# Another order of states, scalings and x operands in the projection phase of the last eight chunks

## The chip, the cores and the metric

The kernel runs on one core of a Trainium2 chip. The metric is device time in microseconds, as the median of three runs of the whole kernel: 601.86 (601.72 to 603.16).

## What is computed

Linear attention with a decay, block by block, feeds a feed-forward layer with a squared ReLU. All inputs and outputs are float32.

```python
# attention: batch 4, heads 8, 768 tokens, 64 per head, blocks of 64
for b in range(nb):
    intra = np.einsum('bhic,bhjc->bhij', qb, kb) * Dmask[None]
    intra = np.einsum('bhij,bhjd->bhid', intra, vb)
    inter = np.einsum('bhid,bhde->bhie', qb * lam_pow[None], kv_state)
    out[:, :, sl] = intra + inter
    kb_dec = kb * rev_pow[None]
    kv_state = lam_block * kv_state + np.einsum('bhsd,bhse->bhde', kb_dec, vb)
# feed-forward: 3072 tokens, d_model 512, d_ff 2048
h = x @ w_in
r = np.maximum(h, 0.0)
return ((r * r) @ w_out).astype(np.float32)
```

## The kernel before

**Tiling.** Tokens go in 24 chunks of 128, six per batch row; a chunk holds all eight heads, two by two in four pairs. Chunks 0 to 7 make the first two groups of the feed-forward, chunks 8 to 15 the next two, chunks 16 to 23 the last two. Every float32 factor of a matrix product is kept as a rounded high part and a remainder (`wh` and `wl`, `gh` and `gl`, `xh` and `xl`), and a product is three matmuls. From the third group on the products go by a scheme with seven products instead of eight (`product`, line 667; `gather`, line 897), which wants sums of blocks of the weights and of x as operands.

**Order.** Nothing is scheduled by a program: each engine runs its instructions in the order in which the code emits them, and waits where an operand is not there. The engines are TensorE (PE), VectorE (DVE), ScalarE (ACT), GpSimd (POOL) and SyncE (SP), which issues the DMAs.

**The projection phase of the last eight chunks** is the loop over f from 0 to 15 behind the `quad` loop. At its start all hidden values of group m are done, and one projection of it is left; those of group m + 1 lie in `gs`. Each step f does one projection (`project`: 24 matmuls from lines 537, 538 and 542 into four `acc` banks). It needs `gh` (ACT, line 960) and `gl` (DVE, line 522), which `again` makes from `gs` one step ahead, in two buffers each. Each even step also does the attention of one chunk t = 16 + f/2, by `go(t, after, apart)`. That is on PE: the old states times the queries (line 442), the scores of chunk t + 1 (line 406), the new parts of the state (`news_of`, line 421) and the masked scores times the values (line 467). Ahead of line 467 stands a copy of one element on ACT, `mark` (line 447): line 467 may add to its bank only when that copy has read it. Behind it ACT copies the result to `packs` (line 478), and DVE masks the scores of t + 1 (`a`).

The state of a chunk has two halves. `state(t, False)` adds the decayed state `kvd` and the new part for the first half of t + 1; `state(t + 1, True)` does the same for its second half; each runs on DVE (`kv`), and POOL then decays the result (`fade_state`, line 496, `kvd`). `scale_q(t + 1)` and `scale_k(t + 2)` are POOL operations on the queries and keys in place (lines 398 and 390). go(t + 1) reads both states, the queries of t + 1 and the keys of t + 2.

Two chunks at a time are also turned into operands x of the next phase: `even` and `last` are the chunks' results as they are, `near` and `far` are sums of DVE. `part_hi` rounds one on ACT (line 631), `part_lo` takes the remainder on DVE (line 635). The last two pairs of `w_out` rows get their sums here: `fold` (DVE: two `rec`, four `sums`), `fold_hi` (ACT, line 694), `fold_lo` (DVE, and two stores `wt` on SP, line 700). After the loop `open_ring` loads the first `ring` tiles, and `quad_all` starts the next phase.

At the very start chunks 0 to 3 are attended while `w_in` is taken apart: `clamp`, `shift`, `sign` and `rounded` are steps of that on DVE, and `masked(3)` makes `a` of chunk 3.

Of the kernel before, what the change touches and what calls it, by code (L numbers as in the profile page):

```python
# [24 lines left out]
NF = DF // P  # L25
# [10 lines left out]
def body(ctx: ExitStack, tc: tile.TileContext, qT, kT, kvq, lam, w, out):  # L36
# [43 lines left out]
    def load_kv(t):  # L80
        if t in (2, 3):
            x = lent[t][:, 1].rearrange("p a b -> p (a b)")
        elif t in lent:
            x = lent[t][:, 1]
        else:
            x = io.tile([P, 2 * DM], F32, name="kv_sb")
        nc.sync.dma_start(out=x, in_=kvq[t, :, 0 : 2 * DM])
        x = x.rearrange("p (k h d) -> p k h d", k=2, h=H)
        tok[t] = x[:, 0], x[:, 1]
# [50 lines left out]
    def sign(u):  # L140
        L, Hw, A = cv[u]
        V.scalar_tensor_tensor(  # L142
            out=A, in0=Hw, scalar=0xC0000000, in1=A, op0=ALU.bitwise_and, op1=ALU.bitwise_or
        )
# [153 lines left out]
    def masked(t):  # L298
        a_of[t] = []
        for j in range(2):  # L300
            a = wk.tile([P, NPR, C], F32, name="a", tag="gl" if t in (1, 3) else "a")
            V.tensor_tensor(
                out=a, in0=sc_of[t][j].rearrange("p (a b) -> p a b", a=NPR),
                in1=mask[:, j], op=ALU.mult,
            )
            a_of[t].append(a)
# [85 lines left out]
    def scale_q(t):  # L392
        x = feat[t][:, 1].rearrange("p a (b c) -> p a b c", b=2)
        if t % NCB:
            y = qpow[:, :, 0:D].unsqueeze(2).broadcast_to([P, NPR, 2, D])
        else:
            x, y = x[:, :, 1], qpow[:, :, 0:D]
        nc.gpsimd.tensor_tensor(out=x, in0=x, in1=y, op=ALU.mult)
# [33 lines left out]
    def go(t, after, apart):  # L432
        o = [ps_a.tile([P, DM], F32, name="att") for _ in range(2)]
        q_, vs = feat[t][:, 1], tok[t][1]
        for g in range(2):
            for p in range(NPR):
                for j, r in enumerate(rows):
                    h = (g + j + 1) % 2
                    if h and not t % NCB:
                        continue  # L440
                    st = kv[:, :, 0:D] if h else kv[:, :, D:]
                    nc.tensor.matmul(  # L442
                        o[h][r, p * D : (p + 1) * D], st[r, p, :], q_[r, p, of_half(h)],
                        start=p == 0, stop=False, skip_group_check=True,
                    )
                    end = h
        nc.scalar.copy(mark[:, 2:3], o[end][D : D + 1, 0:1])
        u = o
        if after is not None:
            scores_by_half(after, ps_h, "h")  # L450
            if apart:
                u = sc_of[after]

        def all_news():
            for p in range(NPR):
                if t % NCB < NCB - 1:
                    news_of(0, t, u[0], p, apart)
                if after is not None:
                    news_of(1, after, u[1], p, apart)

        if apart:
            all_news()
        a = a_of.pop(t)
        for p in range(NPR):
            for h in (end, 1 - end):
                for j, r in enumerate(rows):
                    nc.tensor.matmul(  # L467
                        o[h][r, p * D : (p + 1) * D], vs[rows[h], 2 * p + j, :], a[rows[h], j, p, :],
                        start=p == 0 and h == 1 and not t % NCB, stop=True, skip_group_check=True,
                    )  # L470
        if not apart:
            all_news()
        if after is not None:
            part_of[after] = u[1]
            masked_by_half(after)
        x = kept(t).rearrange("p (a c) -> p a c", a=NPR)
        for h in range(2):
            nc.scalar.copy(x[:, :, of_half(h)], o[h][:, 0 : NPR * D].rearrange("p (a c) -> p a c", a=NPR))
        part_of[t] = u[0]
# [48 lines left out]
    def project(m, f):  # L528
        gh, gl = g_of.pop((m, f))
        if f == 0:  # L530
            accs[m] = [ps_acc.tile([P, DM], F32, name="acc") for _ in range(G)]
        end = f == NF - 1
        j = w_out(f)

        def high(i):
            cs = slice(i * C, (i + 1) * C)
            nc.tensor.matmul(accs[m][i], gh[:, cs], wh[:, j], start=f == 0, stop=False)  # L537
            nc.tensor.matmul(accs[m][i], gh[:, cs], wl[:, j], start=False, stop=False)  # L538

        def low(i):  # L540
            cs = slice(i * C, (i + 1) * C)
            nc.tensor.matmul(accs[m][i], gl[:, cs], wh[:, j], start=False, stop=end)  # L542
            if end:
                if i % 2 == 0:
                    stage.append(wk.tile([P, 2, DM], F32, name="o", tag="A"))
                o = stage[-1][:, i % 2]
                if i % 2:
                    V.tensor_copy(o, accs[m][i])
                else:
                    nc.scalar.copy(o, accs[m][i])  # L550
                t = chunk(m, i)
                nc.sync.dma_start(out=out[t * C : (t + 1) * C, :], in_=o)

        n = 2 if end and m == NM - 1 else 1
        for i in range(0, G, n):
            for step in (high, low):
                for k in range(i, i + n):
                    step(k)
# [78 lines left out]
    def part(*a):  # L637
        part_hi(*a)
        part_lo(*a)

    def even(i, t):
        return i, 0, 4, kept(t)

    def last(i, t):
        return i, 4, 2, kept(t + 1)[:, 2 * C :]
# [33 lines left out]
    def fold(n):  # L679
        rec = wk.tile([P, 2, 2, 2 * P], F32, name="rec", tag="A")  # L680
        for i in range(2):
            j = w_out(2 * n + i)
            add(rec[:, i].rearrange("p b c -> p (b c)"), f32(wh[:, j]), f32(wl[:, j]))
        x = wk.tile([P, 4, 2 * P], F32, name="sums", tag="A")
        (b11, b12), (b21, b22) = ([rec[:, i, j] for j in range(2)] for i in range(2))
        T1, T2, T3, T4 = (x[:, i] for i in range(4))
        sub(T1, b12, b11)
        sub(T2, b22, T1)
        sub(T3, b22, b12)
        sub(T4, b21, T2)  # L690
        FOLD[n] = x

    def fold_hi(n):
        nc.scalar.copy(wh[:, NF - 2 : NF].rearrange("p a d -> p (a d)"), FOLD[n].rearrange("p a b -> p (a b)"))

    def fold_lo(n):
        hi, lo = (t[:, NF - 2 : NF].rearrange("p a d -> p (a d)") for t in (wh, wl))
        sub(lo, FOLD.pop(n).rearrange("p a b -> p (a b)"), f32(hi))
        for i, x in enumerate((hi, lo)):
            nc.sync.dma_start(out=wt[n, :, :, i], in_=f32(x).rearrange("p (a b) -> p a b", a=4))  # L700
# [280 lines left out]
    def att(t, pool, name):  # L981
        o[t] = pool.tile([P, DM], F32, name=name)
        u[t] = pool.tile([P, DM], F32, name=name)
# [21 lines left out]
    masked(2)  # L1005
    clamp(1)
    shift(1)
    sign(1)
    low[1] = split(1, o[1])
    scores(3, ps_acc, "acc")  # L1010
    prep_q(3)
    prep_k(3)
    masked(3)
    att(2, ps_a, "att")
    news(2, u[2])
    faded(2, u[2])
# [90 lines left out]
    def behind(f, t, last):  # L1107
        if f % 2:
            state(t, False)
            if t < last:  # L1110
                scale_q(t + 1)

    def ahead(f, t, last):
        if f % 2 and t < last:
            state(t + 1, True)
            if t + 2 <= last:
                scale_k(t + 2)
# [71 lines left out]
    masked_by_half(first_t)  # L1189
    state(first_t, True)  # L1190
    scale_q(first_t)
    for f in range(NF):
        t = first_t + f // 2
        i, odd_ = f // 4, f // 2 % 2
        project(*prev)
        prev = (m + 1, f)
        if f % 2 == 0:
            KEPT[t] = packs[:, i % 2, odd_]
            go(t, t + 1 if t < last_t else None, t < last_t)
            if t + 3 <= last_t:  # L1200
                load_qk(t + 3)
                load_kv(t + 3)
        if f + 1 < NF:
            again(m + 1, f + 1)
        if f % 2 == 0:
            behind(f + 1, t, last_t)
        else:
            ahead(f, t, last_t)
        if f in (4, 8):
            fold(NF // 2 - 2 + f // 8)  # L1210
        if f in (5, 9):
            fold_hi(NF // 2 - 2 + f // 8)
            fold_lo(NF // 2 - 2 + f // 8)
        if f % 4 == 1:
            part(*even(i, t))
        if f % 4 == 2:
            part(*near(i, t - 1))
        if f % 4 == 3:
            part(*far(i, t - 1))
            part(*last(i, t - 1))  # L1220
    open_ring()
    for n in range(NF // 2):
        quad_all(n, prev)
# [55 lines left out]
```

## Time and profile before

| | |
|---|---|
| median of three runs | 601.86 us |
| the profiled execution, whole | 602.65 us |
| its span, first to last instruction | 600.9 us |
| PE busy | 580.5 us (97%) |
| DVE busy | 421.9 us (70%) |
| ACT busy | 257.7 us (43%) |
| POOL busy | 100.4 us (17%) |
| the phase: go(16) to the first product behind it | 362.82 to 436.35 us |

Times in the profile are microseconds from the start of the span. An engine's idle time is put down to what released it. A matmul's duration in the trace is longer than its distance to the next one, since matmuls are pipelined; for PE the distances between starts tell the pace.

### The profile page before, as it was taken

The numbers are of one execution on the slowest core, as the hardware profiler recorded it, in microseconds if no ns is written. First come the engines' busy times: TensorE is split into PE (matmuls) and PEld (weight loads), VectorE is DVE, ScalarE is ACT, GpSimd is POOL, SyncE is SP. The second block draws the span as 40 slices with busy tenths as digits, with TensorE's granted clock in tenths as the row PEclk, the third lists the DMA queues.
The fourth block names the chain that finished last, engine by engine and source line by source line (L and its number), as shares of the span: only waits on it lengthen the run. The fifth ranks groups of instructions, "written<-read, shape, count | busy, mean of one in ns | idle before, by whom it ended". The sixth has DMA issues, their size and how long they took to land.

```text
span 600.9 us, 12444 instructions
## 1 busy us (share of the span) xinstructions
PE 580.5 (97%) x5006; PEld 491.2 (82%) x5006; DVE 421.9 (70%) x684; ACT 257.7 (43%) x437; POOL 100.4 (17%) x106
## 2 busy tenths in 40 slices
PE   7989999999999999999999999888899999999996
PEld 5777888888888888888888888676788888999996
DVE  6899999947656758566666645878664546997942
ACT  4576877734334455433333323333342323642520
POOL 5421222333323231000000013344200000000000
PEclk9999999999999999999999999999999999999999
DMA  8766576328788692656666555255058666766863
GB/s 299 271 236 211 160 260 212 106 71 289 233 284 270 212 320 81 192 150 195 194 192 194 177 179 183 100 182 171 3 190 291 195 194 181 244 209 211 282 204 114
DMA packets 69385, 119.31 MB, mean 199 GB/s; under 512 B 6352, under 2 KB 30928, under 8 KB 69328
## 3 DMA queue, kind: packets, MB, share of 16 engines
q1 hardware_dynamic: 67152, 116.42, 59.7%
q10 hardware_dynamic: 2176, 2.10, 1.0%
q8 instruction: 40, 0.66, 0.5%
q14 instruction: 17, 0.14, 0.1%
HBM read 88.08 MB, written 29.36 MB: 195 GB/s over the span
## 4 chain that ended last, share of the span: by engine, by line
PE 77%; DVE 12%; ACT 3%; issue 3%; POOL 2%; DMA 2%; SPq 0%; DVEq 0%; POOLq 0%
PE h L667 17%; PE h L507 12%; PE acc L897 7%; PE acc L537 7%; PE acc L542 7%; PE acc L538 7%; PE att L667 7%; PE att L897 4%; PE h L897 2%; PE att L442 2%; PE att L467 1%; DVE A L142 1%; DVE far L212 1%; DVE sums L212 1%; DVE gl L522 1%
## 5 line engine op out<-in xcount | busy, mean ns | idle before, releaser
L537 PE MATMUL acc<-wh,gh 128*128 128x512 f32 x256 | 101.2, 395 | 0.0
L538 PE MATMUL acc<-wl,gh 128*128 128x512 f32 x256 | 99.8, 390 | 0.0
L542 PE MATMUL acc<-wh,gl 128*128 128x512 f32 x256 | 99.8, 390 | 0.0
L667 PE MATMUL h<-wh,ring 128*128 128x512 f32 x320 | 85.9, 390 | 0.0
L514 ACT ACTIVATE h<-h 128x512 f32<-128x512 f32 x48 | 28.0, 583 | 112.2 <-PE h L507 50.7
L667 PEld LDWEIGHTS h<-wh,ring 128*128 128x128 f32 x320 | 59.8, 188 | 13.2 <-DVE kv_sb L212 0.7
L522 DVE TENSOR_TENSOR gl<-h,gh 128x512 fp32r<-128x512 f32 x48 | 33.0, 688 | 39.6 <-ACT h L517 39.6
L537 PEld LDWEIGHTS acc<-wh,gh 128*128 128x128 f32 x256 | 48.0, 188 | 11.0 <-issue 0.3
L542 PEld LDWEIGHTS acc<-wh,gl 128*128 128x128 f32 x256 | 48.0, 188 | 10.6 <-DVE gl L522 0.5
L538 PEld LDWEIGHTS acc<-wl,gh 128*128 128x128 f32 x256 | 48.1, 188 | 9.6
L667 PE MATMUL h<-wl,ring 128*128 128x512 f32 x160 | 49.3, 389 | 0.0
L496 POOL TENSOR_TENSOR kvd<-kv,qpow 128x256 f32<-128x256 f32 x27 | 22.5, 833 | 114.8 <-DVE kv L212 94.3
L390 POOL TENSOR_TENSOR kv_sb<-kv_sb,mask 128x512 f32<-128x512 f32 x14 | 19.2, 1373 | 125.3 <-DMA kv_sb<-in_kvq 125.2
L507 PE MATMUL h<-xh,wh 128*128 128x512 f32 x128 | 35.9, 402 | 0.1
L897 PE MATMUL acc<-folds,wh 128*128 128x256 f32 x192 | 35.2, 283 | 0.0
L667 PEld LDWEIGHTS h<-wl,ring 128*128 128x128 f32 x160 | 30.0, 188 | 6.2
L507 PE MATMUL h<-xh,wl 128*128 128x512 f32 x128 | 34.5, 391 | 0.4 <-DVE wl L157 0.4
L507 PE MATMUL h<-xl,wh 128*128 128x512 f32 x128 | 34.2, 389 | 0.0
L667 PE MATMUL att<-wh,ring 128*128 128x512 f32 x128 | 34.2, 389 | 0.0
L212 DVE TENSOR_TENSOR wl<-sums,wh 128x1024 fp32r<-128x1024 f32 x24 | 30.0, 1252 | 2.2 <-ACT wh L869 1.8
L897 PEld LDWEIGHTS acc<-folds,wh 128*128 128x128 f32 x192 | 30.0, 192 | 0.0
L516 ACT ACTIVATE gh<-h 128x512 fp32r<-128x512 f32 x48 | 28.8, 600 | 1.5
(251 smaller groups left out, 1188.8 us busy)
## 6 DMA issues: line engine op xcount, KB each, us to landing
ring<-ws SPq DMA_DIRECT2D x112, 256.0 KB, 3.0
raw<-in_w SPq DMA_DIRECT2D x32, 512.0 KB, 4.5
folds<-wt SPq DMA_DIRECT2D x64, 256.0 KB, 3.7
kv_sb<-in_kvq SPq DMA_DIRECT2D x20, 512.0 KB, 6.0
ws<-parts SPq DMA_DIRECT2D x32, 256.0 KB, 3.8
qk_sb<-in_kT SPq DMA_DIRECT2D x20, 256.0 KB, 4.0
qk_sb<-in_qT SPq DMA_DIRECT2D x20, 256.0 KB, 4.6
out_x<-o SPq DMA_DIRECT2D x16, 256.0 KB, 2.3
```

The source lines that it names most:

```text
L212: lambda o, x, y, op=op: V.tensor_tensor(out=o, in0=x, in1=y, op=op)
L390: nc.gpsimd.tensor_tensor(out=x, in0=x, in1=y.broadcast_to([P, NPR, 2, D]), op=ALU.mult)
L496: nc.gpsimd.tensor_tensor(out=kvd, in0=d, in1=qpow[:, :, D - 1 : D].broadcast_to([P, NPR, D]), op=ALU.mult)
L507: nc.tensor.matmul(h, wt[:, f, kt * P : (kt + 1) * P], x[:, kt], start=k == 0, stop=k == 11)
L514: nc.scalar.activation(h, h, AF.Relu)
L516: nc.scalar.activation(gh, h, AF.Square)
L522: V.tensor_tensor(out=gl, in0=r, in1=gh.bitcast(F32), op=ALU.subtract)
L537: nc.tensor.matmul(accs[m][i], gh[:, cs], wh[:, j], start=f == 0, stop=False)
L538: nc.tensor.matmul(accs[m][i], gh[:, cs], wl[:, j], start=False, stop=False)
L542: nc.tensor.matmul(accs[m][i], gl[:, cs], wh[:, j], start=False, stop=end)
L667: nc.tensor.matmul(bank, x[:, part_, kt], t[:, q + kt], start=start and z == 0, stop=stop and z == 5, skip_group_check=True,)
L897: nc.tensor.matmul(bank[:, r * 2 * P : (r + 1) * 2 * P], x, y, start=n == 0 and r == 0 and z == 0, stop=n == NQ - 1 and z == 2, skip_group ...
```

## The change

In the phase above each even step now emits, right behind `go(t)`, `scale_q(t + 1)` and `state(t, False)`, ahead of `again`, and behind `again` `state(t + 1, True)` and `scale_k(t + 2)`. Before, the first two stood behind `again` of the even step and the last two behind `again` of the odd step. The x operands are put on a list (`late`) and come one step later: their rounding ahead of the next operands' sums, their remainder behind. The w_out sums move from steps 4, 5 and 8, 9 to steps 8, 9 and 12, 13. At the start `sign(1)` goes behind `masked(3)`.

```diff
@@ -1005,12 +1005,12 @@
     masked(2)
     clamp(1)
     shift(1)
-    sign(1)
     low[1] = split(1, o[1])
     scores(3, ps_acc, "acc")
     prep_q(3)
     prep_k(3)
     masked(3)
+    sign(1)
     att(2, ps_a, "att")
     news(2, u[2])
     faded(2, u[2])
@@ -1189,35 +1189,47 @@
     masked_by_half(first_t)
     state(first_t, True)
     scale_q(first_t)
+    late = []
     for f in range(NF):
         t = first_t + f // 2
         i, odd_ = f // 4, f // 2 % 2
+        more = t < last_t
         project(*prev)
         prev = (m + 1, f)
         if f % 2 == 0:
             KEPT[t] = packs[:, i % 2, odd_]
-            go(t, t + 1 if t < last_t else None, t < last_t)
+            go(t, t + 1 if more else None, more)
+            if more:
+                scale_q(t + 1)
+                state(t, False)
             if t + 3 <= last_t:
                 load_qk(t + 3)
                 load_kv(t + 3)
+        now, late = late, []
         if f + 1 < NF:
             again(m + 1, f + 1)
-        if f % 2 == 0:
-            behind(f + 1, t, last_t)
-        else:
-            ahead(f, t, last_t)
-        if f in (4, 8):
-            fold(NF // 2 - 2 + f // 8)
-        if f in (5, 9):
-            fold_hi(NF // 2 - 2 + f // 8)
-            fold_lo(NF // 2 - 2 + f // 8)
+        if f % 2 == 0 and more:
+            state(t + 1, True)
+            if t + 2 <= last_t:
+                scale_k(t + 2)
+        for x in now:
+            part_hi(*x)
         if f % 4 == 1:
-            part(*even(i, t))
+            late.append(even(i, t))
         if f % 4 == 2:
-            part(*near(i, t - 1))
+            late.append(near(i, t - 1))
         if f % 4 == 3:
-            part(*far(i, t - 1))
-            part(*last(i, t - 1))
+            late.append(far(i, t - 1))
+            late.append(last(i, t - 1))
+        for x in now:
+            part_lo(*x)
+        if f in (8, 12):
+            fold(NF // 2 - 4 + f // 4)
+        if f in (9, 13):
+            fold_hi(NF // 2 - 4 + f // 4)
+            fold_lo(NF // 2 - 4 + f // 4)
+    for x in late:
+        part(*x)
     open_ring()
     for n in range(NF // 2):
         quad_all(n, prev)
```

DVE, from the masked scores that go(20) makes: `a`, the two states `kv`, the conversions `gl`, the w_out sums (`rec`, `sums`). Before:

```order
L212 TENSOR_TENSOR a<-h,mask 128x256 x2
L522 TENSOR_TENSOR gl<-gs,gh 128x512
L212 TENSOR_TENSOR kv<-kvd,h 128x4x64
L212 TENSOR_TENSOR rec<-wh,wl 128x512 x2
L212 TENSOR_TENSOR sums<-rec 128x256
L212 TENSOR_TENSOR sums<-rec,sums 128x256
L212 TENSOR_TENSOR sums<-rec 128x256
L212 TENSOR_TENSOR sums<-rec,sums 128x256
L522 TENSOR_TENSOR gl<-gs,gh 128x512
L212 TENSOR_TENSOR kv<-kvd,h 128x4x64
L212 TENSOR_TENSOR wl<-sums,wh 128x1024
```

After:

```order
L212 TENSOR_TENSOR a<-h,mask 128x256 x2
L212 TENSOR_TENSOR kv<-kvd,h 128x4x64
L522 TENSOR_TENSOR gl<-gs,gh 128x512
L212 TENSOR_TENSOR kv<-kvd,h 128x4x64
L635 TENSOR_TENSOR wl<-far,wh 128x4x128
L635 TENSOR_TENSOR wl<-packs,wh 128x2x128
L212 TENSOR_TENSOR rec<-wh,wl 128x512 x2
L212 TENSOR_TENSOR sums<-rec 128x256
L212 TENSOR_TENSOR sums<-rec,sums 128x256
L212 TENSOR_TENSOR sums<-rec 128x256
L212 TENSOR_TENSOR sums<-rec,sums 128x256
L522 TENSOR_TENSOR gl<-gs,gh 128x512
```

Both states now stand ahead of the w_out sums, and two operand remainders stand between.

ACT, around the same w_out sums: `gh` conversions, the rounding of the sums (line 694) and the next mark. Before, from go(20) on:

```order
L478 COPY packs<-att 128x4x64 x2
L960 CAST gh<-gs 128x512 x2
L694 CAST wh<-sums 128x1024
L631 CAST wh<-packs 128x4x128
L447 COPY mark<-att 1x1
L478 COPY packs<-att 128x4x64 x2
```

After:

```order
L478 COPY packs<-att 128x4x64 x2
L960 CAST gh<-gs 128x512
L631 CAST wh<-far 128x4x128
L631 CAST wh<-packs 128x2x128
L960 CAST gh<-gs 128x512
L694 CAST wh<-sums 128x1024
L447 COPY mark<-att 1x1
L478 COPY packs<-att 128x4x64 x2
```

The rounding of `even` (line 631, from `packs`) is gone from the rows ahead of the mark, the rounding of `far` and `last` stands behind go(20)'s copies, and the rounding of the sums stands right ahead of the mark of go(21).

POOL, behind go(19) and go(20): the decays of the states (`kvd`), the queries (line 398) and the keys (line 390). Before:

```order
L496 TENSOR_TENSOR kvd<-kv,qpow 128x256
L398 TENSOR_TENSOR qk_sb<-qk_sb,qpow 128x512
L496 TENSOR_TENSOR kvd<-kv,qpow 128x256
L390 TENSOR_TENSOR lent<-lent,mask 128x512
L496 TENSOR_TENSOR kvd<-kv,qpow 128x256
L398 TENSOR_TENSOR lent<-lent,qpow 128x512
```

After:

```order
L398 TENSOR_TENSOR qk_sb<-qk_sb,qpow 128x512
L496 TENSOR_TENSOR kvd<-kv,qpow 128x256 x2
L390 TENSOR_TENSOR lent<-lent,mask 128x512
L398 TENSOR_TENSOR lent<-lent,qpow 128x512
L496 TENSOR_TENSOR kvd<-kv,qpow 128x256 x2
L390 TENSOR_TENSOR kv_sb<-kv_sb,mask 128x512
L398 TENSOR_TENSOR qk_sb<-qk_sb,qpow 128x512
```

The queries come ahead of the two decays, and both decays and the keys stand in one row.

## Rows read from the trace of the kernel before

**Rows 1.** the page: busy time, one DVE group (total us, mean ns):

```profile
PE 580.5 (97%) x5006; PEld 491.2 (82%) x5006; DVE 421.9 (70%) x684; ACT 257.7 (43%) x437; POOL 100.4 (17%) x106
...
L212 DVE TENSOR_TENSOR wl<-sums,wh 128x1024 fp32r<-128x1024 f32 x24 | 30.0, 1252 | 2.2 <-ACT wh L869 1.8
```

**Rows 2.** PE's waits, 379.22 to 436.35: total us, times, longest:

```profile
PE att L442 <- DVE kv L212: 3.4, 4, 1.6
...
PE h L421 <- POOL kv_sb L390: 2.5, 3, 1.1
...
PE att L467 <- ACT mark L447: 2.5, 4, 0.7
```

**Rows 3.** timeline of PE: start us, us, instruction, idle before in brackets:

```profile
362.82 1.08 PE L442 MATMUL att<-qk_sb,kv 64*64 64x64 f32 x28
...
364.68 0.22 PE L467 MATMUL att<-a,kv_sb 64*64 64x64 f32 x1
...
365.37 0.50 PE L537 MATMUL acc<-wh,gh 128*128 128x512 f32 x1
...
379.22 0.90 PE L442 MATMUL att<-lent,kv 64*64 64x64 f32 x15
...
394.08 0.50 PE L537 MATMUL acc<-wh,gh 128*128 128x512 f32 x1
...
399.74 0.32 PE L442 MATMUL att<-qk_sb,kv 64*64 64x64 f32 x2
...
431.48 1.15 PE L442 MATMUL att<-qk_sb,kv 64*64 64x64 f32 x32
...
433.50 0.50 PE L537 MATMUL acc<-wh,gh 128*128 128x512 f32 x1
...
436.35 1.07 PE L667 MATMUL h<-wh,ring 128*128 128x512 f32 x4
```

**Rows 4.** timeline of DVE, the same columns:

```profile
364.95 0.76 DVE L212 TENSOR_TENSOR a<-h,mask 128x256 f32<-128x256 f32 x2 [1.51 <-PE h L421]
...
366.71 0.69 DVE L522 TENSOR_TENSOR gl<-gs,gh 128x512 fp32r<-128x512 f32 x1 [1.00 <-ACT gh L960]
...
368.89 1.34 DVE L522 TENSOR_TENSOR gl<-gs,gh 128x512 fp32r<-128x512 f32 x1 [1.16 <-ACT gh L960]
...
370.15 0.41 DVE L212 TENSOR_TENSOR kv<-kvd,h 128x256 f32<-128x256 f32 x1
...
386.68 1.51 DVE L212 TENSOR_TENSOR sums<-rec 128x256 f32<-128x256 f32 x1
...
388.22 0.43 DVE L212 TENSOR_TENSOR sums<-rec,sums 128x256 f32<-128x256 f32 x1
```

**Rows 5.** timeline of POOL, the same columns:

```profile
367.81 0.62 POOL L496 TENSOR_TENSOR kvd<-kv,qpow 128x256 f32<-128x256 f32 x1 [5.04 <-DVE kv L212]
...
368.39 1.30 POOL L398 TENSOR_TENSOR qk_sb<-qk_sb,qpow 128x512 f32<-128x512 f32 x1
```

**Rows 6.** timeline of ACT, the same columns:

```profile
389.35 1.05 ACT L694 CAST wh<-sums 128x1024 fp32r<-128x1024 f32 x1 [3.01 <-DVE sums L212]
```

**Rows 7.** timeline of SP's DMA issues, 410 to 446, the same columns:

```profile
413.59 0.52 SPq L700 DMA_DIRECT2D wt<-wl  x1
...
415.79 27.50 SPq L653 DMA_DIRECT2D ring<-ws  x10
```

**Rows 8.** DMA issues, 405 to 422: count, KB each, median us to landing:

```profile
ring<-ws SPq DMA_DIRECT2D x4, 256.0 KB, 3.7
```

**Rows 9.** timeline of DVE near the start, the columns of rows 3:

```profile
21.72 1.96 DVE L142 SCALAR_TENSOR_TENSOR A<-raw,A 128x1024 uint32<-128x1024 uint32 x1
...
37.22 1.23 DVE L142 SCALAR_TENSOR_TENSOR A<-raw,A 128x1024 uint32<-128x1024 uint32 x1
```

**Rows 10.** PE's waits, 18 to 42, the columns of rows 2:

```profile
PE att L314 <- POOL kv_sb L296: 1.7, 1, 1.7
...
PE acc L322 <- DVE a L302: 1.1, 2, 0.9
```

## The prediction

> **What bounds the kernel now.** I read the page first: TensorE (PE) is busy 97% of the 600.9 us span, so a gain must come from PE idle time or from work dropped, and this change drops none [rows 1]. PE's waits inside the stretch from the attention step of chunk 18 to the end of the phase name three kinds, 8.4 us in all: a state (`kv`), a scaled key (`kv_sb`) and ScalarE's (ACT's) mark [rows 2]. The timeline of PE gives what they cost with refilling [rows 3]. In what follows go(t) is PE's attention step of chunk t; it runs at even f and is followed by two projections. Undisturbed, go(16) takes 365.37 - 362.82 = 2.55 us. Two projections take 399.74 - 394.08 = 5.66 us, disturbed or not. So an undisturbed round is 8.2 us. But go(18) to go(20) is 399.74 - 379.22 = 20.52, where two rounds would be 16.4, and go(20) to the first product of the next phase is 436.35 - 399.74 = 36.61; it holds four go's, three pairs of projections and a single one.
>
> Who ends last there? A go(t+1) needs both states of go(t), the scaled queries of t+1 and the scaled keys of t+2. All their inputs exist when go(t) ends. Before, they stand on VectorE (DVE) and GpSimd (POOL) behind the two conversions `gl`, the `near`/`far` sums and the w_out sums, and so come up to 1.6 us late.
>
> **Part 1, states and scalings sooner.** All is counted from the first matmul of a go. In go(16) `a` (the two masked scores) starts at 364.95 - 362.82 = 2.13 and DVE is free 0.7 later [rows 3, 4]. The first state follows at once and is done at 3.2. POOL scales the queries from 1.7 to 3.0 (1.30), then fades the state (0.62) to 3.9 [rows 5]. `gl` (0.69) runs to 4.5, the second state (0.41) to 4.9 [rows 4], POOL fades to 5.5 and scales keys to 6.8. The next go starts at 8.2: every item is 1.4 us or more ahead. `gl` of step f+1, which now stands behind one state, is needed in the second projection, from 2.55 + 2.83 = 5.4 on, and ends at 4.5. So the waits on `kv` and `kv_sb` go to zero. The queries are scaled in place after the scores have read them, so POOL cannot start before 1.7; that is in the walk. No DMA is added. The loads go out in the same steps; those of chunk 22 move ahead of the w_out store, which held the SP queue.
>
> **Part 2, x operands one step later.** ACT's mark stood behind the `far` cast, which waited for DVE; the far cast now comes one step later, behind the mark. The 0.73 waits at go(18), go(20), go(22) go. With 16 instead of 32 state matmuls go(18) should take some 2.35. To the start of go(20): 2.35 + 5.66 + 2.55 + 5.66 = 16.2 instead of 20.52, a gain of **4.3**.
>
> **Part 3, the w_out sums (steps 8, 9 and 12, 13).** Here a new wait arises. First the row: `gl` at 368.89 takes 1.34 beside POOL's scaling (368.39 to 369.69) instead of 0.69, while the state at 370.15, with one input in PSUM, takes its usual 0.41; a `sums` takes 1.51 instead of 0.43 [rows 4, 5]. So DVE operations with two SBUF inputs stand still beside POOL; I let them alternate with it whole. [...] If they merely shared, the wait at go(21) below would vanish and the store behind it come 1.5 us sooner: about 592.
>
> From the start of go(20): second state to 4.85; `far` remainder to 5.4; POOL's fade to 6.0; the next remainder to 6.3; POOL's key scaling to 7.2; two `rec` (about 0.6 each) to 8.35; four `sums` (0.34 from start to start) to 9.75. POOL's query scaling of go(21) asks at 8.2 + 1.7 = 9.9, just too late to block them. ACT rounds the sums (1.05) [rows 6] to 10.8. Only then comes the mark of go(21), which ACT has queued behind this cast, and PE's last matmuls of go(21) start at 10.95 instead of 8.25 + 1.86 = 10.1 (364.68 - 362.82 = 1.86 in go(16) [rows 3]): a new wait of **0.8**. Before, the mark stood behind this cast and an `even` cast too, but in go(21) PE waited longer for its states anyway. go(21) then ends at 11.6. On DVE: `gl` to 10.3, POOL to 11.25, remainder of the sums (1.25 [rows 1]) to 12.3, `a` to 13.0, states to 14.9, `near`, `even`, `gl` to 18.1, `far` to 19.1, POOL, `near` remainder to 20.6, `a` to 21.3, states to 23.2, `far` remainders to 24.0, second w_out sums to 26.6. go(22) starts at 17.3 undisturbed, go(23) at 25.6. The mark of go(23) waits for the second ACT cast to 27.7; go(23), 433.50 - 431.48 = 2.02 long before [rows 3], ends about 28.4 where 27.6 was due: **0.8** more.
>
> **The ring.** The queue behind this chain is SP's. The first four loads of `ring`, which feed the next phase, stood at 415.79, twenty us ahead of need, right behind the second w_out store at 413.59 [rows 7]. They stay behind it, and it now waits for the remainder of the second sums, done at 28.9. The store's issue takes 0.52, so the first load starts at 29.5. The four took a median 3.7 us to land behind such a store [rows 8]: 33.2. The last projection ends at 28.4 + 2.83 = 31.2, so product 0 waits about **2.1**. The x operands are nearer than that: `even` remainder at 31.6, `near` 33.2, both before PE asks. go(20) to product 0 becomes 33.3 instead of 36.61, a gain of **3.3**; bounds: 29.6 (no wait at all, gain 7.0) and 36.6 (gain 0).
>
> **Part 4, the fourth chunk's mask.** `sign` (1.96) stands ahead of `a` on DVE, and PE waits 1.1 for `a` [rows 9, 10]. It is long because POOL scales beside it. Swapped, `a`, with an input in PSUM, runs beside POOL, and `sign` comes after it, at the 1.23 of the like operation at 37.22 [rows 9]. PE gains 1.1 at once, but then it waits 1.7 for POOL's `kv_sb` [rows 10], which waits for DVE; so what stays is what DVE's chain gains, 1.96 - 1.23 = **0.7** (0 to 1.1). From there to the last phase PE has nearly no waits, so it is carried.
>
> **Sum.** 4.3 + 3.3 + 0.7 = 8.3 us. The profiled execution took 602.65 (1.75 around its span) and would take 594.3; the median of the runs shown, 601.86, becomes **593.6**. The bounds: everything hidden 4.3 + 7.0 + 1.1 = 12.4 (589.5); nothing in the last part and at the front 4.3 (597.6).
>
> **Rivals.**
> *The last part is wholly hidden.* If DVE meets POOL less often than I let it, both marks are in time, and the ring loads go out some 2 us sooner and land with the last projection: 2.1 + 1.6 - 0.8 of rest, near 3 us more gain, 590.6. For it: DVE's own work from go(20) to the second sums' remainder (three `a`, six states, six `gl`, six remainders, `near`, `far`, two w_out sums at plain durations) is about 20 of the 28.9 us. Against: before, the same operations were stretched as assumed. 0.20.
> [...] 0.20.
> *It does not do what it says.* PE's states arrive sooner, but DVE is the bound and takes the gain back: not under 599.9. Against: DVE's plain work from go(18) to the second store (29 us, counted the same way) and POOL's (five query scalings, nine fades, four key scalings, 16.6 us), if never overlapped, take 45.6 us, and product 0, some 4.4 us behind, starts at 50 instead of 57.13. 0.06.
> *Slower.* `gl` now stands behind a state on DVE, and POOL scales and fades in the same 5 us. If `gl` ended later than 5.4 from a go's start, PE would stand in every second projection. It ends at 4.5; a query scaling in front (1.30) takes it 0.4 over the edge, which in seven go's is 2.8 us. It would need two of them, 1.5 us of wait in each, 10.5 in all: 604. For it: only the 1.34 of the one stretched `gl`. 0.05.
>
> **How the numbers follow.** Forecast 593.6 with 0.49; its own range is 592 to 595.2. The two rivals beside it carry the range to 590.4 and 597.4. Faster by over 0.3% (under 600.05; about what a measurement here can tell from no change) takes the forecast and the first two rivals: 0.89. Within 0.3%: 0.06. Slower: 0.05.
>
> **What would show it.** PE's waits on `kv` and on `kv_sb`/`lent` in the phase gone; go(18) to go(20) near 16.2 us; waits on the mark left at go(21) and go(23) only, each behind the rounding of w_out sums on ACT; PE waiting on a `ring` DMA ahead of the next phase's first product; PE's wait on `a` near 24 us gone and the one on `kv_sb` near 40 us come 0.7 earlier. Wrong would be: `gl` as a releaser of PE, a query load not landed when POOL asks, or a landing of `ring` past 36 us from go(20).

## The result, and the profile after

| | before | after |
|---|---|---|
| median, runs beside each other | 602.51 us (601.72 to 603.34) | 596.11 us (594.88 to 597.87) |
| ratio, 95% interval | | 0.9896, 0.9863 to 0.9928 |
| the profiled execution | 602.65 us | 596.83 us |
| its span | 600.9 us | 594.8 us |
| the phase, go(16) to the first product behind it | 73.53 us | 66.28 us |

The change makes the kernel 1.0% faster. The forecast of 593.6 lay 2.5 us below the median, and the range of 590.4 to 597.4 held it. The median of before is 602.51 here and not the 601.86 that the forecast started from, so the gain is 6.4 us where 8.3 was forecast. A second set of runs of the same kernel (e0_after below) had a median of 594.97. Ratios here and below are taken over the fast runs and need not equal the quotient of the medians, and one run of e3_sign_only, of 1471.76 us, stands outside its ratio.

First the waits of PE in 355 to 440 of after (engine and line, what it waited for, total us, times, longest us):

```profile
PE att L467 <- ACT mark L447: 2.7, 2, 1.9
PE h L667 <- DMA ring<-ws: 1.6, 1, 1.6
```

The waits on states (`kv`) and scalings (`kv_sb`, `lent`) of [rows 2] are gone; four of the mark became two, and a new one on the ring stands at the phase's end. The timeline of PE gives their places (start us, us, instruction, idle before it in brackets):

```profile
380.22 0.90 PE L442 MATMUL att<-lent,kv 64*64 64x64 f32 x15
...
396.34 1.08 PE L442 MATMUL att<-qk_sb,kv 64*64 64x64 f32 x29
...
404.49 1.08 PE L442 MATMUL att<-lent,kv 64*64 64x64 f32 x29
...
407.39 0.69 PE L467 MATMUL att<-a,lent 64*64 64x64 f32 x32 [0.82 <-ACT mark L447]
...
421.83 1.15 PE L442 MATMUL att<-qk_sb,kv 64*64 64x64 f32 x32
424.86 0.69 PE L467 MATMUL att<-a,kv_sb 64*64 64x64 f32 x32 [1.88 <-ACT mark L447]
425.49 0.50 PE L537 MATMUL acc<-wh,gh 128*128 128x512 f32 x1
...
430.14 1.17 PE L667 MATMUL h<-wh,ring 128*128 128x512 f32 x4 [1.62 <-DMA ring<-ws]
```

go(18) starts at 380.22, go(20) at 396.34, go(21) at 404.49, go(23) at 421.83, and the first product at 430.14. Against [rows 3], go(18) to go(20) is 16.12 us instead of 20.52, and go(20) to the product 33.80 instead of 36.61.

Why the marks come late stands in the rows of DVE, ACT and POOL behind go(20) and go(22) (columns as above):

```profile
402.47 2.15 DVE L212 TENSOR_TENSOR rec<-wh,wl 128x512 f32<-128x512 f32 x2
...
405.67 0.42 DVE L212 TENSOR_TENSOR sums<-rec,sums 128x256 f32<-128x256 f32 x1
...
415.64 1.77 DVE L635 TENSOR_TENSOR wl<-near,wh 128x512 fp32r<-128x512 f32 x1
...
423.14 0.42 DVE L212 TENSOR_TENSOR sums<-rec,sums 128x256 f32<-128x256 f32 x1
```

```profile
406.12 1.04 ACT L694 CAST wh<-sums 128x1024 fp32r<-128x1024 f32 x1 [3.79 <-DVE sums L212]
407.19 0.15 ACT L447 COPY mark<-att 1x1 f32<-1x1 f32 x1
...
423.59 1.04 ACT L694 CAST wh<-sums 128x1024 fp32r<-128x1024 f32 x1 [3.92 <-DVE sums L212]
424.66 0.15 ACT L447 COPY mark<-att 1x1 f32<-1x1 f32 x1
```

```profile
402.23 1.24 POOL L390 TENSOR_TENSOR kv_sb<-kv_sb,mask 128x512 f32<-128x512 f32 x1
406.23 1.58 POOL L398 TENSOR_TENSOR qk_sb<-qk_sb,qpow 128x512 f32<-128x512 f32 x1 [2.76 <-PE h L406]
```

The first w_out sums end 9.75 us behind go(20), the second 27.2. Each time ACT rounds them, and only then takes the mark. SP's queue stands behind the same chain:

```profile
425.92 0.51 SPq L700 DMA_DIRECT2D wt<-wl  x1
426.54 5.57 SPq L653 DMA_DIRECT2D ring<-ws  x5
```

**The account of the two profiled executions.** The span is cut at the first scores (line 283), at chunk 4's first line 314, at go(16), and at the first product. The stretches differ by +1.89, -0.87, +0.02, -7.25 and, behind the product, +0.10 us; together -6.1. So the phase gave 7.25 and the front 0.87. The first stretch lost 1.89: after's first scores start at 10.80, before's at 8.91. The change touches nothing there. PE does the same 14 matmuls of line 251 in each. The row of before, then that of after:

```profile
7.10 1.88 PE L251 MATMUL h<-pz 128*128 128x128 f32 x14 [1.59 <-DVE pz L232]
```

```profile
7.58 3.29 PE L251 MATMUL h<-pz 128*128 128x128 f32 x14 [1.14 <-DVE pz L232]
```

They took 3.29 us instead of 1.88, which is 1.41 of the 1.89; the rest lies ahead of them. The views print a granted clock of 1.00 for both, but the trace of after has no record of PE's clock before 10.68 us, where those matmuls end, and before's record starts at 4.42. Ahead of that first record a matmul of line 251 takes 0.42 us (the one at 5.80 in after), behind it 0.28 (the one at 5.23 in before). That makes PE's clock the likely cause; no record shows it directly. Of the eleven other profiles of this study's kernels, before's among them, ten take 1.88 us for the fourteen matmuls, as before does (first scores at 8.75 to 8.95), and one (e8_sums_behind_gl, 3.36 us, first scores at 10.44) begins as after does. This goes with the run, and not with the kernel.

### The profile page after: what moved, and what is told of

Its sections match the earlier page's. It is cut to its first block, busy times and chain, and to the rows that moved or that the text cites. A ratio compares the mean times of both kernels' runs of the same rounds, so it can differ in the third digit from the quotient of the medians.

```text
span 594.8 us, 12455 instructions
## 1 busy us (share of the span) xinstructions
PE 579.9 (97%) x5006; PEld 491.2 (83%) x5006; DVE 416.1 (70%) x684; ACT 258.1 (43%) x437; POOL 98.4 (17%) x106
## 4 chain that ended last, share of the span: by engine, by line
PE 82%; DVE 7%; DMA 5%; issue 2%; ACT 2%; POOL 1%; SPq 0%; POOLq 0%; DVEq 0%; ACTq 0%
PE h L667 17%; PE h L507 12%; PE acc L537 8%; PE acc L542 8%; PE acc L538 8%; PE acc L897 7%; PE att L667 7%; PE att L897 4%; PE att L442 2%; PE h L897 2%; DMA qk_sb<-in_kT 2%; PE att L467 1%; DMA kv_sb<-in_kvq 1%; PE h L406 1%; DMA ws<-wh 1%
## 5 line engine op out<-in xcount | busy, mean ns | idle before, releaser
L390 POOL TENSOR_TENSOR kv_sb<-kv_sb,mask 128x512 f32<-128x512 f32 x14 | 17.5, 1251 | 124.5 <-DMA kv_sb<-in_kvq 120.9
```

The lines of the kernel that those rows point to most:

```text
L390: nc.gpsimd.tensor_tensor(out=x, in0=x, in1=y.broadcast_to([P, NPR, 2, D]), op=ALU.mult)
```

## The experiments

The first three take the change apart, from before. The fourth repeats it. The rest start from after, and move or take away what still waits. A phase is always go(16) to the first product.

### One part alone: states and scalings

```diff
             go(t, t + 1 if t < last_t else None, t < last_t)
+            if t < last_t:
+                scale_q(t + 1)
+                state(t, False)
...
-        if f % 2 == 0:
-            behind(f + 1, t, last_t)
-        else:
-            ahead(f, t, last_t)
+        if f % 2 == 0 and t < last_t:
+            state(t + 1, True)
+            if t + 2 <= last_t:
+                scale_k(t + 2)
```

> The kernel before with the states and scalings emitted right behind go, as in the change; x operands, w_out sums and sign stay where they were. The phase from go(16) to the first product took 73.5 us before and 66.3 after the change; undisturbed it would be 62.1. Theory (two separate causes, states and ACT's queue): the waits of PE on kv and kv_sb go, three waits on the mark behind the far cast (about 1.1 each with refilling) and two behind the w_out sums (about 0.8 each) stay, no wait on the ring: 67 us, 6.5 us off the whole time. Rival (the late operands are what frees the chain, the place of the states is secondary): 71 us or more.

Measured: 598.65 us beside 602.87 of before, ratio 0.9945 (0.9924 to 0.9965); phase 69.16 us. The waits of PE in the phase are of one kind:

```profile
PE att L467 <- ACT mark L447: 6.5, 6, 2.4
```

So the waits on states and scalings go with this part alone, and the mark takes part of the gain back: 6.5 us where before had 2.5 [rows 2]. ACT at go(19) shows what the mark stands behind:

```profile
388.49 1.05 ACT L694 CAST wh<-sums 128x1024 fp32r<-128x1024 f32 x1 [3.93 <-DVE sums L212]
389.44 0.61 ACT L631 CAST wh<-packs 128x512 fp32r<-128x512 f32 x1
390.08 0.15 ACT L447 COPY mark<-att 1x1 f32<-1x1 f32 x1
```

The phase lies between the two theories; neither number was met. The theory's mechanism held: the old waits go, the marks stay, the ring does not wait. Its size for the marks did not: it had 4.9 us (three of 1.1, two of 0.8), and the phase is 7.1 above the undisturbed 62.1.

### The other part alone: x operands and w_out sums

```diff
+        now, late = late, []
...
+        for x in now:
+            part_hi(*x)
         if f % 4 == 1:
-            part(*even(i, t))
+            late.append(even(i, t))
...
-        if f in (4, 8):
-            fold(NF // 2 - 2 + f // 8)
...
+        if f in (8, 12):
+            fold(NF // 2 - 4 + f // 4)
```

> The kernel before with the x operands one step later and the w_out sums in steps 8, 9, 12, 13, states and scalings and sign in their old places. Theory: the mark waits behind the far cast go, but kv and kv_sb still come late (about 1 us in each of go(19), go(20), go(22), 3 us in go(21), where the w_out sums stand ahead of the second state), and the wait on the ring appears (about 2 us): phase about 70 us, 3.5 off the whole time. Rival: 67 us, if the operands were the cause.

Measured: 602.21 us, ratio 0.9988 (0.9971 to 1.0004): no difference that shows. The phase is 72.96 us, and both theories asked for less. PE's waits there:

```profile
PE att L442 <- DVE kv L212: 5.3, 4, 2.5
```

The marks are nearly in time (0.3 us), but the second state of each chunk still stands at the end of DVE's row, and the sums come ahead of it, now with the operand remainders of the step before in front of them. DVE behind go(20):

```profile
403.03 2.38 DVE L212 TENSOR_TENSOR rec<-wh,wl 128x512 f32<-128x512 f32 x2
...
406.80 0.69 DVE L522 TENSOR_TENSOR gl<-gs,gh 128x512 fp32r<-128x512 f32 x1
407.40 0.41 DVE L212 TENSOR_TENSOR kv<-kvd,h 128x256 f32<-128x256 f32 x1
```

The state ends at 407.81, and go(21) begins its main part at 407.87 after a wait of 2.51. go(23) has another, of 2.48. Behind both PE's granted clock fell to 0.50 (stretch, its us, busy time of PE, PEld, DVE, ACT, POOL, then the granted clock, DMA share, GB/s):

```profile
408.00:410.00 2.00, 2.00 (x54) 2.00 (x58) 1.59 (x1) 0.08 (x1) 2.00 (x2) 0.50 0.46 154
...
432.00:434.00 2.00, 2.00 (x6) 1.52 (x5) 0.97 (x2) 1.51 (x4) 0.00 (x0) 0.50 1.03 343
```

The round of go(21) took 12.27 us instead of 8.15, 1.6 more than its wait explains, and the stretch from go(23) to the product 9.25 instead of the 4.95 of e4_old_steps below, 1.8 more than its wait. The first part gives 4.37 us of phase, this one 0.57, both 7.25. The waits of PE themselves add up: they are 8.8 us in all before, 6.5 with the first part alone, 6.4 with this one and 4.3 with both. So what this part alone lacks is, as far as these rows tell, mostly the half clock behind the two waits that it leaves.

### The swap at the start alone

```diff
     shift(1)
-    sign(1)
     low[1] = split(1, o[1])
...
     masked(3)
+    sign(1)
```

> The kernel before with only sign(1) behind masked(3). From the first scores to the first matmul of chunk 4's state: 32.20 us before, 31.33 after the change. Theory: 31.3 here too, 0.9 us off the whole time, phase unchanged at 73.5. Rival (the front gain came from the later first scores): 32.2, no change. The first scores start at 8.9 us (before) or 10.8 (after): theory, it varies from run to run and not with the kernel.

Measured: 602.27 us, ratio 0.9984 (0.9966 to 1.0001). First scores to chunk 4's line 314 is 31.31 us where before had 32.20; the phase, 73.49, is untouched. The mechanism shows in DVE's rows, `a` ahead and `sign` (line 142) short:

```profile
21.62 1.27 DVE L302 TENSOR_TENSOR a<-acc,mask 128x512 f32<-128x512 f32 x2
22.82 1.21 DVE L142 SCALAR_TENSOR_TENSOR A<-raw,A 128x1024 uint32<-128x1024 uint32 x1
```

The size is less sure than this one profile says. In e1_states_only, with the old order, the same stretch was 31.44, in e2_operands_only 32.20. With the new order it lies between 31.25 and 31.68 in nine profiles. In e0_after `sign` took 2.12 us, and the stretch was 31.27 nonetheless. The row ahead of `sign` explains most of it: `shift` (line 135). Before, then e1_states_only:

```profile
20.03 1.66 DVE L135 TENSOR_SCALAR A<-A 128x1024 uint32<-128x1024 uint32 x1
```

```profile
19.85 0.69 DVE L135 TENSOR_SCALAR A<-A 128x1024 uint32<-128x1024 uint32 x1
20.58 2.18 DVE L142 SCALAR_TENSOR_TENSOR A<-raw,A 128x1024 uint32<-128x1024 uint32 x1
```

Two scalings of POOL run there, and each holds up a `shift` or `sign` that it meets. Before and in e2_operands_only they met both (1.66 and 1.96 in before, 0.69 and 1.21 where they are not held); in e1_states_only only `sign` was held. With the new order they never hold more than one of the two: `shift` here and in after, `sign` in e0_after (where `shift` took 0.69). So the swap is worth 0.9 us where both would be held, and 0.1 to 0.2 where POOL meets `sign` alone. In the three profiles at 31.66 to 31.68 neither is held, and what sets that stretch stays open.

### The change once more

> The changed kernel again, beside the next three on one chip. Theory: phase 66.3 within 0.2, whole time 6 to 8 us under before; the start of the first scores is either about 8.9 or about 10.8, and the whole time follows it.

Measured: 594.97 us (594.75 to 595.38) beside 603.40 of before, ratio 0.987 (0.9852 to 0.9889): 8.4 us by the medians. First scores at 8.75 us, phase 66.57. So the slow first 10 us are not the kernel's. The wait on the mark of go(23) is again 1.89 us, but what follows differs. The granted clock of 422 to 426 in this run, then of 426 to 428 in after (columns as above):

```profile
422.00:424.00 2.00, 1.27 (x33) 1.15 (x34) 1.25 (x2) 0.82 (x3) 0.00 (x0) 0.72 0.14 51
424.00:426.00 2.00, 2.00 (x5) 1.54 (x6) 0.96 (x2) 1.52 (x4) 0.00 (x0) 0.50 1.09 385
```

```profile
426.00:428.00 2.00, 2.00 (x10) 1.60 (x10) 1.14 (x3) 1.31 (x3) 0.00 (x0) 1.00 1.09 386
```

Here PE's granted clock fell to 0.50 after 1.9 us of idleness, and the first matmuls of the last projection took 0.63 us each instead of 0.39 (a projection is 12 matmuls, not the 24 of the section on the kernel before, and about half of them ran so). The phase is only 0.3 longer, because the ring ends last: PE waited 0.32 for it instead of 1.62.

### The w_out sums back in their old steps

```diff
-        if f in (8, 12):
-            fold(NF // 2 - 4 + f // 4)
-        if f in (9, 13):
-            fold_hi(NF // 2 - 4 + f // 4)
-            fold_lo(NF // 2 - 4 + f // 4)
+        if f in (4, 8):
+            fold(NF // 2 - 2 + f // 8)
+        if f in (5, 9):
+            fold_hi(NF // 2 - 2 + f // 8)
+            fold_lo(NF // 2 - 2 + f // 8)
```

> The changed kernel with the w_out sums back in steps 4, 5 and 8, 9. Theory: the wait on the ring (1.6) goes, as the second store now goes out some 17 us sooner; the mark waits stand at go(19) and go(21), 0.8 to 1.2 each, in place of 0.8 and 1.9: phase 64.2, 2 us less than the changed kernel. Rival (the later steps are needed to relieve DVE early on): 66.3 or more, with waits on kv back at go(19).

Measured: 597.51 us, ratio 0.9911 (0.9886 to 0.9935); phase 69.20. The theory fell. The ring's wait is gone, as expected of sums this early, but go(21), at 404.45, waits 3.18 us for its mark. The rows of DVE, POOL, ACT and PE:

```profile
403.83 2.15 DVE L212 TENSOR_TENSOR rec<-wh,wl 128x512 f32<-128x512 f32 x2
...
406.35 1.39 DVE L212 TENSOR_TENSOR sums<-rec,sums 128x256 f32<-128x256 f32 x1
```

```profile
406.19 1.26 POOL L398 TENSOR_TENSOR qk_sb<-qk_sb,qpow 128x512 f32<-128x512 f32 x1 [1.36 <-PE h L406]
```

```profile
408.44 1.04 ACT L694 CAST wh<-sums 128x1024 fp32r<-128x1024 f32 x1 [6.15 <-DVE sums L212]
```

```profile
409.71 1.13 PE L467 MATMUL att<-a,lent 64*64 64x64 f32 x32 [3.18 <-ACT mark L447]
```

The sums of step 4 and their remainder had already pushed DVE back, so `rec` starts 1.4 us later than in after, and POOL's query scaling of go(21) now catches a `sums`, which takes 1.39 instead of 0.42. The sums end 12.1 us behind go(20) instead of 9.75. This crosses the margin of the prediction's Part 3, which had sums that end at 9.75 and a query scaling that asks at 9.9. And the wait costs about twice its length. The windows behind it (columns as above):

```profile
410.00:412.00 2.00, 2.00 (x35) 1.69 (x31) 1.73 (x4) 1.09 (x4) 0.19 (x1) 0.50 0.69 247
...
414.00:416.00 2.00, 2.00 (x6) 1.58 (x5) 1.88 (x2) 0.13 (x1) 1.33 (x2) 0.50 1.01 288
```

The round of go(21) takes 14.44 us instead of 8.15. Of the 6.29, 3.18 are the wait; the other 3.1 go with the clock of 0.50 behind it.

### The first ring loads ahead of the store

```diff
+    def open_first():
+        ring[:] = [wk.tile([P, 4, DM], F32R, name="ring", tag="raw")]
+        for k in range(4):
+            stream(k)
...
+        if f == 12:
+            open_first()
```

> The changed kernel with the first four ring loads emitted in step 12, ahead of the second w_out store on the SP queue. Theory: PE's wait of 1.6 us on the ring goes, the next limit being the even remainder, ready about 0.4 us ahead of its matmul: phase 64.7. Rival (the DVE chain holds product 0 as well): 66.3 less a few tenths, with a wait on wl.

Measured: 594.03 us, ratio 0.9856 (0.9834 to 0.9879), 0.9 us under e0_after of the same chip, whose runs overlap with these; phase 66.06. Rows of SP, then of PE:

```profile
409.40 1.41 SPq L653 DMA_DIRECT2D ring<-ws  x1
```

```profile
422.83 0.97 PE L467 MATMUL att<-a,kv_sb 64*64 64x64 f32 x32 [1.88 <-ACT mark L447]
...
427.85 1.07 PE L677 MATMUL h<-wh,ring 128*128 128x512 f32 x4
```

The last of the four loads goes out at 409.40, and the product (here line 677) no longer waits for the ring, so the order on SP's queue was that wait's whole cause. But the phase is only 0.2 us shorter than after's and 0.5 shorter than e0_after's. The granted clock fell in this run too (0.77 from 422 to 424, 0.50 from 424 to 426), and the first half of the last projection ran at about half pace (0.63 us a matmul instead of 0.39), now with nothing beside it to hide that. The theory's 64.7 left this out.

### The keys of chunk 22 unscaled

This kernel leaves out POOL's scaling of the keys of chunk 22.

```diff
-            if t + 2 <= last_t:
+            if t + 2 <= last_t and t + 2 != last_t - 1:
                 scale_k(t + 2)
```

> The changed kernel without the scaling of chunk 22's keys (left out: POOL's operation that runs beside the first w_out sums). Theory (POOL and a DVE operation with two SBUF inputs exclude each other): the two rec of step 8 take 1.3 instead of 2.15, the sums come 0.9 sooner, and the mark wait of 0.8 at go(21) goes. Rival (the rec are long for another reason): 2.15 and 0.8 stay.

Measured, one run: 595.41 us, phase 66.53. DVE behind go(20), which here starts at 394.92, 1.4 us earlier on the axis than in after:

```profile
401.05 1.28 DVE L212 TENSOR_TENSOR rec<-wh,wl 128x512 f32<-128x512 f32 x2
```

`rec` takes 1.28 instead of 2.15, so the other 0.87 were time in which it stood still for the POOL operation. The mark of go(21) is in time but for some 0.2 us, and the round of go(21) takes 8.33 instead of 9.20. The phase as a whole is no shorter than that of e0_after: the mark of go(23) now costs 2.1 us and the granted clock falls behind it (0.59 from 424 to 426, 0.56 from 426 to 428). The prediction's Part 3 let the two engines take turns, and priced the case that they merely share. The first of the two `rec` of after alone speaks for turns:

```profile
402.47 1.55 DVE L212 TENSOR_TENSOR rec<-wh,wl 128x512 f32<-128x512 f32 x1
```

It ends 0.55 us behind the key scaling (402.23 and 1.24 make 403.47), and two undisturbed `rec` take 1.28, so it did nearly all its work once POOL was done.

### The sums two steps apart from their rounding

Two kernels start from after with the sums in earlier steps and their rounding behind the next go, so that no mark stands behind it. In the first the sums stand ahead of the next `gl`, in the second behind it.

```diff
-        if f in (8, 12):
-            fold(NF // 2 - 4 + f // 4)
-        if f in (9, 13):
-            fold_hi(NF // 2 - 4 + f // 4)
-            fold_lo(NF // 2 - 4 + f // 4)
+        if f in (4, 8):
+            fold(NF // 2 - 2 + f // 8)
+        if f in (6, 10):
+            fold_hi(NF // 2 - 2 + f // 8)
+            fold_lo(NF // 2 - 2 + f // 8)
```

> The changed kernel with the w_out sums in steps 4 and 8 and their rounding and remainder behind the go of steps 6 and 10, so that no mark stands behind them. Theory: no mark wait at go(19), go(21) or go(23) but the old 0.25, no ring wait: phase 62.5, 3.8 us under the changed kernel, and the best of all. Rival: DVE, with the remainder (1.2) ahead of the conversions, makes gl late and PE waits on gl instead: 64 or more.

Measured: 592.82 us, ratio 0.9831 (0.9809 to 0.9853), 2.15 us under e0_after, which ran beside it; phase 64.04 where the theory had 62.5. This is faster than before and after. The marks and the ring are in time but for 0.3 us; a `gl` isn't:

```profile
PE acc L542 <- DVE gl L522: 1.5, 1, 1.5
```

It stands behind the `rec` and `sums` of step 8 on DVE, and PE's first projection behind go(21) needs it. One of these sums is again held by POOL's query scaling (405.94 to 407.30):

```profile
406.20 1.38 DVE L212 TENSOR_TENSOR sums<-rec,sums 128x256 f32<-128x256 f32 x1
```

That is 0.96 of the 1.5. The next kernel has the sums behind `gl` (the first kernel ran again beside it).

```diff
-        if f in (4, 8):
+        if f in (5, 9):
             fold(NF // 2 - 2 + f // 8)
```

> The same kernel as e6_cast_behind, beside the next one on one chip. Theory: ratio to before 0.983, phase 64.0 us, one wait of PE of 1.5 us on gl in the round of go(21). If that wait was a chance of one profile, it is absent here and the phase is near 62.3.

> As e6_cast_behind, but the w_out sums stand behind the conversion gl of the next step (steps 5 and 9) instead of ahead of it. Theory: PE's 1.5 us wait on gl was DVE's queue alone, so it goes; seven rounds of 8.15 and 4.95 behind give a phase of 62.0 to 62.5 us, with neither a mark, nor a gl, nor a ring wait over 0.4; the median is 1.5 to 2 us under e6's of the same call. Rival: the sums, 0.7 us later, now meet POOL's query scaling of go(21), and one of them is held for its 1.25 us; the mask of chunk 22 and the states behind it come late, PE waits on a or kv instead, and the phase stays within 0.7 us of e6's.

Measured: e6_again 593.03 us, 0.9842 (0.9822 to 0.9861), phase 64.05, and the same wait of 1.5. e8_sums_behind_gl 593.16 us, 0.9838 (0.9822 to 0.9854), phase 64.17. The rival held in its size and in the sum that is held, but PE waits on `gl` and not on `a` or `kv`. Rows of DVE, then of POOL, in the second kernel:

```profile
403.81 1.54 DVE L522 TENSOR_TENSOR gl<-gs,gh 128x512 fp32r<-128x512 f32 x1
...
406.48 1.50 DVE L212 TENSOR_TENSOR sums<-rec 128x256 f32<-128x256 f32 x1
```

```profile
403.57 1.24 POOL L390 TENSOR_TENSOR kv_sb<-kv_sb,mask 128x512 f32<-128x512 f32 x1
406.07 1.64 POOL L398 TENSOR_TENSOR qk_sb<-qk_sb,qpow 128x512 f32<-128x512 f32 x1 [1.26 <-PE h L406]
```

Now `gl` meets the key scaling (1.54 instead of 0.69) and a `sums` the query scaling (1.50 instead of 0.42). DVE is late in the rounds of go(21) and go(22) (8.97 and 9.61 us instead of 8.15), and PE waits three times for a `gl`, 1.4 us in all. In these two kernels moving the sums moved the wait and did not end it.

## Why the prediction was right, and where it wasn't

**Part 1 and Part 2 held.** The waits on states and scalings went, `gl` released no wait of PE in after's phase, and go(18) to go(20) came out at 16.12 us for a forecast 16.2. The gain there is 4.40 us for 4.3. e1_states_only and e2_operands_only show that neither part alone gives it.

**Part 3 held in its mechanism.** The first sums end 9.75 us behind go(20), as the walk had it, and the mark of go(21) costs 0.82 for 0.8. The alternation of DVE with POOL on which the walk rests is shown by e7_no_keys_22 (two `rec` in 1.28 us instead of 2.15). The step that was too small is the mark of go(23): 1.88 us of wait for 0.8. The second sums end at 27.2 instead of 26.6; 0.5 of that is there when the `near` remainder beside POOL ends (415.64 and 1.77, 21.1 behind go(20) for 20.6). The rest is mostly the base: the 2.02 us of go(23) that I took for its plain length [rows 3] already held 0.24 of wait, since line 467 could have started 1.15 us after the step began (424.86 - 1.88 - 421.83), and it took 0.63 more. The store and the first ring load came 0.7 us later than forecast (30.2 for 29.5 behind go(20)). The ring's wait, 1.62 for 2.1, was smaller because the projection ahead of it ended later: two late chains side by side, of which one counts. So go(20) to the product gained 2.81 for 3.3, 0.5 short.

**Part 4** was 0.7, and 0.87 in the profiled pair. Its mechanism was half of it: POOL also holds `shift`, which has one input (1.66 us instead of 0.69), and which of the two operations is held changes from run to run. In e1_states_only most of it (0.76) came without the swap, so its share of the median stays open.

**The sum** was 8.3. The profiled pair gave 4.40 + 2.81 + 0.87 and 0.04 ahead of go(18), 8.1 us; the slow first stretch and 0.1 at the end took 2.0 back. The second set of runs gave 8.4. What the first set's gain of 6.4 lacks is thus not in the phase. A first stretch like after's accounts for 1.9; whether the other runs of that set began so too isn't recorded. The sum had no term for such a stretch, and that it came out at 8.4 in the second set holds two misses that cancel in part, the mark of go(23) too small and the ring too large.

**The rivals.** Not wholly hidden: both marks and the ring did wait. The query scaling did not catch the last `sums` in after, though by little: they end at 406.09 and the scaling starts at 406.23. e4_old_steps, e6_cast_behind and e8_sums_behind_gl are on the other side of that edge, the first 2.5 us above e0_after (on another chip). The upper end of the range, 597.4, and a chance of 0.20 were the author's estimate for w_out sums that end later than Part 3 has them. No run of after's order shows that; in e4_old_steps, where they do end later, PE waited 3.18 us and the phase was 2.9 longer than after's. No `gl` came late in after; in e6_cast_behind one did, and cost 1.5 us. The rival that is slower priced two query scalings at 1.5 us of wait; its own row gives 1.7 (4.5 and twice 1.30, less 5.4), which changes nothing, as none came.

**Left out of the prediction** was what a wait of PE costs beyond its length: at 3.18 us another 3.1 (e4_old_steps), at 2.51 and 2.48 some 1.6 and 1.8 (e2_operands_only), at 1.88 and 1.89 some 1.4 to 1.6 in two runs (from line 467 of go(23) to the end of the last projection 5.02 and 5.21 us, e5_ring_first and e0_after) and nothing in a third (3.66, after).

## What to carry to other kernels

Put on each engine first what the next step of the bound engine needs, and let copies for later phases stand behind the mark or state that someone waits for. Do not judge one half of such a change by its time alone: e2_operands_only took 2.3 us of waits away and gained nothing, because the granted clock fell to 0.50 behind the waits that were left. Where a trace shows two engines taking turns (here DVE and POOL: two `rec` in 2.15 us instead of 1.28), count each operation in full against the other's, and look for the place where a few tenths decide which of two operations goes first. Expect a large operation that is moved to take its wait along unless the round that it goes to has room. Where a short copy that releases the bound engine stands behind a long rounding, put the rounding after it: e6_cast_behind, which does that with the sums made earlier, gained 2.15 us on top of the change.

## What the runs showed of the hardware

- PE's granted clock fell to 0.50 in stretches of 2 us around waits of PE of 3.18 us (e4_old_steps), 2.51 and 2.48 (e2_operands_only), 1.89 (e0_after) and 1.88 (e5_ring_first), and to 0.59 and 0.56 behind one of 2.13 (e7_no_keys_22). It stayed at 1.00 in after's profile, with the same 1.88 at the same place, and in e1_states_only with 2.39, so the length of a wait alone does not decide it here. Matmuls of 512 columns then took 0.63 us instead of 0.39, for some 2 to 5 us.
- At the start a matmul of line 251 took 0.42 us ahead of the trace's first record of the clock and 0.28 behind it; that record came at 4.42 us in before and at 10.68 in after. The slow start varies between runs of one kernel: fourteen of these matmuls took 1.88 us in e0_after and 3.29 in after. What decides it these runs don't show.
- Beside a POOL operation DVE stood still with two inputs in SBUF (a `gl` 1.54 us instead of 0.69, a `sums` 1.50 instead of 0.42, e8_sums_behind_gl) and with `shift`, which has one (1.66 instead of 0.69, before and e1_states_only). With one of two inputs in PSUM it did not: in after the two `a` and the state behind them at 390.32 took their usual 0.76 and 0.41 beside the query scaling of 389.94 to 391.22.
